# Block 0's logit sums through DRAM instead of TensorE, in a two-layer attention and GLU kernel

## The chip, the core and the metric

The kernel runs on one core of a Trainium2 chip. The metric is the device time of one execution in microseconds (us), the median of several runs. One further execution is recorded by the profiler; all traces below are of that one.

## What is computed

Two layers, with the same weights in both, on x of 2048 rows by 1024 in bfloat16. Each is an attention over a dilated window and then a gated unit:

```python
# _A_ref: H = 32 heads of Dh = 32, window W = 8, dilation 2
qkv = (x @ wqkv)                                  # split in q, k, v per head
idx = pos[:, None] - (jnp.arange(W) * 2)[None, :] # masked where idx < 0
logits = einsum("bhsd,bhswd->bhsw", q, kg) * Dh ** -0.5
o = einsum("bhsw,bhswd->bhsd", softmax(logits), vg)
return o.reshape(B, S, D) @ wo
# _B_ref: gate = x @ W_gate; up = x @ W_up
# h = (gate * (gate > 0)) * up; return h @ W_down      (F = 3584)
x = x + _A_ref(_layernorm(x)); x = x + _B_ref(_layernorm(x))     # twice
```

A logit is thus, for each row, head and one of 8 window places, a sum of 32 products q times shifted k.

## The kernel before

**Blocks.** The 2048 rows go in four blocks of 512 (b = 0 to 3, four tiles of 128 rows each). A stage of a layer is done block by block: normalize and transpose the rows (xnT, by DMA transposes on SyncE's queue, L278), project to q, k, v (`plan_proj`, L386; the projection runs weight-stationary, so its results have features on the partitions and rows along the free axis), attention on VectorE (`plan_attn`, L554), the wo product (`plan_wo`, L697) and the gated unit (`plan_gu`, L724, and `plan_down`, L765). TensorE (PE) does all large products; the attention's logits and weighted sums are done by VectorE (DVE) from copies of q, k and v that went through DRAM (q_d, k_d, v_d) and came back head-major: partition = head + 32 x tile, with the 32 features of that head and 128 rows of the tile along the free axis (qhm, khm, vhm, loaded by SyncE, L562).

**Block 0's logits of layer 0 are special** (`first_logits`, L462), since they have no time for that round trip. Its weights are read with a stride (L397), so that feature chunk c (c = 0 to 7) puts four features of each head on the partitions 4 x head to 4 x head + 3. ScalarE (ACT) copies each chunk of q and k from PSUM to q_fm and k_fm. VectorE multiplies a chunk for all 8 window places at once (`mul`, 128x4096, L496) and adds the chunks in two float32 accumulators of 128x2048, one for each half h of the window (`add`, L506). What is left is the sum over the four partitions of a head. Before the change, TensorE does it: the accumulator is split in bfloat16 terms (`split`, a cast on ScalarE, L515; `rest`, the remainder on VectorE, L528), and `red` (L537) multiplies chunk 7's product and three terms by `wide`, a 128x32 matrix of ones and zeros that GpSimd builds (L186 to L190), in 32 matmuls. ScalarE copies the sums to the logits tile L (L544). `later_hooks` sets these matmuls into block 1's projection, after the first group of ("v", 1) (L551). Then come the softmax (`soft_a`, L597, with the mask of the first rows at L601; `expo` on ScalarE, L609; `soft_b`, L611) and eight pairs of `pv_mul` and `pv_add` (L622, L631), whose outputs GpSimd (POOL) sends to o_d (L638). SyncE loads them back as oT (L646), the operand of wo.

**Order.** It is written out by a planner, not by the engines. `Plan` gives each step a planned time: TensorE's groups follow each other at 0.216 us a matmul (`on_pe`); VectorE's work is either in a chain, with a duration and a time at which it may start (`chain`), or fixed (`on_dve`), as the additions of wo's sums to x (L713) and the multiplications of the gated unit; all steps are then recorded in the order of their planned times (L119). Each engine executes its own queue strictly in that recorded order. Semaphores make what is not ready wait, and with it all that stands behind it on that engine. SyncE's queue holds weight loads, transposes and head-major loads in one line.

**Around the change.** While TensorE projects blocks 1, 2 and 3 of layer 0, VectorE does block 0's logits, softmax and weighted sums, and then block 1's logits, window place by window place (one multiply L576, three additions L586, a fold L593 and L594). `wo_hook` (L815) puts block 0's wo product into the projection of block 3, after group 2 of ("k", 0). Its eight groups of eight matmuls fill the eight PSUM buffers; VectorE adds them to x (L713), ScalarE takes sums and sums of squares of each row tile (L239, L240), VectorE and GpSimd work out mean and scale, ScalarE normalizes (L272) and SyncE transposes two row tiles at a time (L278). The result, xnT of (1, 0), is the operand of the gated unit's first group, the first work of TensorE after block 3's projection. All of block 0's gated unit needs all four row tiles of it.

**Buffers.** `ring` has five slots of 8x512 columns for weights; k's first weights fill two, the wo halves two others, and the gated unit's first gate and up weights go into slots as they come free. The pool `hm` has one buffer for each of the tags q, k and v. The tag "T" has four buffers, for xnT, for oT and for block 0's two accumulators.

Of the kernel before, what the change touches and what calls it, by code (L numbers as in the profile page):

```python
# [9 lines left out]
BF16 = mybir.dt.bfloat16  # L10
# [4 lines left out]
P = 128  # L15
D = 1024
# [107 lines left out]
def kernel(  # L124
# [42 lines left out]
    neg_half = const.tile([P, TPB], F32, name="neg_half")  # L167
    zpad = const.tile([P, KC, HALO], BF16, name="zpad")
    maskc = const.tile([32, W, HALO], F32, name="maskc")
    wide = const.tile([P, H], BF16, name="wide")  # L170
    ring = wring.tile([P, 8 * RING, SLAB], BF16, name="ring")
    q_d = [dram.tile([D, BLK], BF16, name=f"q_d{b}") for b in range(NB)]
    k_d = [dram.tile([D, ROW], BF16, name=f"k_d{b}") for b in range(NB)]
    v_d = [dram.tile([D, ROW], BF16, name=f"v_d{b}") for b in range(NB)]
    o_d = [dram.tile([TPB, H, DH, P], BF16, name=f"o_d{b}") for b in range(NB)]
    x_blk = [xpool.tile([P, TPB, D], BF16, name=f"xb{b}") if b else None for b in range(NB)]
    x_tiles = [x_blk[t // TPB][:, t % TPB, :] if t >= TPB else xpool.tile([P, D], BF16, name=f"x{t}") for t in range(NT)]
# [5 lines left out]
        nc.gpsimd.memset(neg_half[:], -0.5)  # L183

    def consts_late():
        nc.gpsimd.memset(wide[:], 1.0)  # L186
        nc.gpsimd.affine_select(out=wide[:], in_=wide[:], pattern=[[-FG, H]], compare_op=ALU.is_ge,
                                fill=0.0, base=0, channel_multiplier=1)
        nc.gpsimd.affine_select(out=wide[:], in_=wide[:], pattern=[[FG, H]], compare_op=ALU.is_ge,
                                fill=0.0, base=FG - 1, channel_multiplier=-1)  # L190
        nc.gpsimd.memset(zpad[:], 0.0)
        for t in (v_d, k_d):
            nc.gpsimd.dma_start(_dram(t[0], 0, [[ROW, P], [P * ROW, KC], [1, HALO]]), zpad[:])
        nc.gpsimd.memset(maskc[:], 0.0)
        for w in range(1, W):
            nc.gpsimd.memset(maskc[:, w, 0:DIL * w], NEG)
# [261 lines left out]

    def first_logits(st, tm):  # L462
        hold = {}
        terms = []

        def begin():
            hold["q"] = hm_pool.tile([P, KC, BLK], BF16, tag="q", name="q_fm")
            hold["k"] = hm_pool.tile([P, KC, HALO + BLK], BF16, tag="k", name="k_fm")
            nc.gpsimd.memset(hold["k"][:, :, 0:HALO], 0.0)

        def evict(nm, c, acc, t):
            def f():
                if nm == "q":
                    nc.scalar.copy(hold["q"][:, c, :], acc()[:])
                    return
                kt = hold["k"]
                nc.scalar.copy(kt[:, c, HALO:HALO + BLK], acc()[:])
                nc.gpsimd.dma_start(_dram(k_d[1], c * ROW, [[D // P * ROW, P], [1, HALO]]),
                                    kt[:, c, BLK:BLK + HALO])
            if nm == "q" and c == 0:  # L480
                plan.at(t - 1.0, begin)
            plan.at(t, f)
            if nm == "k":
                plan.chain.append((lambda: t + 0.7, 2.3, mul(c), None))
                for h in range(2 if 0 < c < KC - 1 else 0):
                    plan.chain.append((lambda: 0.0, 2.3, add(c, h), split(0, h) if c == KC - 2 else None))
                if c == KC - 1:
                    for n in range(2):
                        for h in range(2):
                            plan.chain.append((lambda n=n, h=h: tm[("split", n, h)], 2.3, rest(n, h),  # L490
                                               split(1, h) if n == 0 else (lambda now: tm.__setitem__("logits", now))))

        def mul(c):
            def f():
                pr = at_pool.tile([P, W, BLK], BF16, tag="pr", name=f"prod_{c}", bufs=2)
                nc.vector.tensor_tensor(pr[:], _ap(hold["q"], c * BLK, [[0, W], [1, BLK]]),  # L496
                                        _ap(hold["k"], c * ROW + HALO, [[-DIL, W], [1, BLK]]), op=ALU.mult)
                hold[("pr", c)] = pr
            return f

        def add(c, h):
            def f():
                if c == 1:
                    hold[("acc", h)] = tpose.tile([P, W // 2, BLK], F32, tag="T", name=f"lacc{h}")
                acc, ws = hold[("acc", h)], slice(4 * h, 4 * h + 4)
                nc.vector.tensor_tensor(acc[:], hold[("pr", 0)][:, ws] if c == 1 else acc[:], hold[("pr", c)][:, ws], op=ALU.add)  # L506
            return f

        def split(n, h):

            def f():
                if h == 0:
                    terms.append(at_pool.tile([P, W, BLK], BF16, tag="pr", name="term_0", bufs=2) if n == 0 else
                                 hm_pool.tile([P, W, BLK], BF16, tag="k", name="term_1"))
                nc.scalar.copy(terms[n][:, 4 * h:4 * h + 4], hold[("acc", h)][:])  # L515

            def after(now):
                t = max(now + 0.2, tm.get(("split", n, 0), 0.0))
                plan.at(t, f)
                tm[("split", n, h)] = t + 2.4  # L520
            return after

        def rest(n, h):
            def f():
                acc = hold[("acc", h)]
                if n == 1 and h == 0:
                    terms.append(hm_pool.tile([P, W, BLK], BF16, tag="q", name="term_2"))
                nc.vector.tensor_tensor(acc[:] if n == 0 else terms[2][:, 4 * h:4 * h + 4], acc[:],  # L528
                                        terms[n][:, 4 * h:4 * h + 4], op=ALU.subtract)
            return f  # L530

        def red():
            Ls = hold["L"] = [psum.tile([P, 4, P], F32, tag="acc", name=f"L{wh}") for wh in range(2)]
            for n, term in enumerate([hold[("pr", KC - 1)]] + terms):
                for wh in range(2):
                    for tq in range(TPB):
                        nc.tensor.matmul(Ls[wh][32 * tq:32 * tq + 32, :, :], lhsT=wide[:],  # L537
                                         rhs=term[:, 4 * wh:4 * wh + 4, tq * P:(tq + 1) * P],
                                         start=(n == 0), stop=(n == 3), skip_group_check=True, tile_position=(0, 32 * tq))

        def out():
            st["L"] = at_pool.tile([P, W, P], F32, tag="L", name="L_0_0")
            for wh in range(2):
                nc.scalar.copy(st["L"][:, 4 * wh:4 * wh + 4, :], hold["L"][wh][:])  # L544

        def step():
            e = plan.on_pe(9.5, red)
            plan.at(e + T_EV, out)
            tm["logits_in"] = e + T_EV + 1.5

        return {"evict": evict}, {("v", 1, 0): step}  # L551


    def plan_attn(L, b, ends, st, tm):  # L554
# [121 lines left out]
            plan.at(t + 0.2, expo)  # L676
            tm["exp"] = t + 2.2

        plan.chain.append(((lambda: tm["logits_in"]) if first else now, 3.0, soft_a, after_a))
        plan.chain.append((lambda: tm["exp"], 4.0, soft_b, None))  # L680

        def after_pv(t):
# [128 lines left out]
    wo_start = []  # L811
    attn = {}
    glu = {}
    later_hooks = []
    wo_hook = {("k", 0, 2): lambda: wo(0, 0)}  # L815

    def proj(L, b):
        st, tm = {}, {}
        if L == 0 and b == 0:
            hooks, later_hooks[:] = (lambda h: (h[0], [h[1]]))(first_logits(st, tm))  # L820
        else:
            hooks = later_hooks.pop() if later_hooks else wo_hook if L == 0 and b == NB - 1 else {}
        attn[(L, b)] = plan_attn(L, b, plan_proj(L, b, hooks), st, tm)

    def wo(L, b):
# [16 lines left out]
    for nm, at in (("q", -6.0), ("k", -5.5)):  # L842
        full = whole[nm].rearrange("p (c a) n -> p c (a n)", c=KC)
        hs = {"last": 0.0}
        plan.reserved.update({0: hs, 1: hs} if nm == "k" else {})
        for g in range(2):
            w0[(nm, g)] = {"t": full, "c0": g * SLAB, "all": hs, "last": 0.0}
            col0 = "qkv".index(nm) * D
            plan.at(at, lambda w=full, c=col0, a=KC // 2 * g, z=KC // 2 * (g + 1):
                    nc.sync.dma_start(w[:, a:z, :], wqkv_v[:, a:z, c:c + D]))  # L850
    w0[("v", 0)] = {"t": held[:, 2 * KC:3 * KC, :], "last": 0.0}
    for h in range(2):
        plan.at(-7.0 + 0.6 * h, lambda a=KC // 2 * h, z=KC // 2 * (h + 1):
# [2 lines left out]
    for t, at in ((1, -6.7), (2, -6.3), (3, -6.2)):  # L856
        plan.at(at, load_x(t))
    plan.at(22.0, consts_late)
    for b, n, at in ((1, 4, -5.7), (2, 4, -2.5), (3, 2, 45.0)):
        for i in range(0, TPB, n):  # L860
            plan.at(at, lambda b=b, n=n, i=i: nc.sync.dma_start(  # L861
                x_blk[b][:, i:i + n, :], _dram(x_dram, (b * BLK + i * P) * D, [[D, P], [P * D, n], [1, D]])))

    for b in range(NB):
        if b == 0:
            late_ln(0, 1, 9.0, on_vector=True)
            late_ln(0, 2, 37.0)
            late_ln(0, 3, 75.5, on_vector=True, norm_at=87.0)
        proj(0, b)
    for b in range(NB):  # L870
        if b >= 1:
# [53 lines left out]
```

## Time and profile before

| | us |
|---|---|
| median of 3 runs | 1620.91 (1620.82 to 1621.05) |
| the profiled execution, device time | 1621.7 |
| its span, first to last instruction | 1620.0 |
| TensorE (PE) busy | 1609.8 |
| VectorE (DVE) busy | 1060.6 |
| ScalarE (ACT) busy | 450.5 |
| GpSimd (POOL) busy | 111.1 |

The granted TensorE clock is 1.000 throughout. The page tells busy time over the whole span; the timelines tell, for one engine, when an instruction started, how long it took, its line and tiles, and in square brackets how long its engine stood idle before it and what ended the wait. SPq and ACTq are the queues of SyncE and ScalarE as they issue DMAs; the landing of a DMA is told by the view of a tile, as time from the issue. The chain of waits goes back from the last instruction to what released each.

### The profile page before, as it was taken

The page shows a single profiled execution, that of the slowest core. Times are in us where ns is not written, and L with a number is a line of the kernel's source. Part 1 is how long each engine was busy: PE and PEld are TensorE (multiplying, and loading weights), DVE is VectorE, ACT ScalarE, POOL GpSimd, SP SyncE. Part 2 cuts the span into 40 slices and gives each one's busy share as a digit, 9 for nine tenths or more (in the row PEclk, how much of TensorE's full clock was granted, in tenths as well). Part 3 has the DMA queues.
Part 4 walks back from the last instruction along what each step waited for, and adds up shares of the span by engine and source line. Part 5 has one row for each costly group of instructions (what it writes and reads, how often), then busy time and mean ns, then how long its engine had stood idle before and what let it go on. Part 6 is the DMA issues. An engine that isn't in the chain of part 4 may idle for free.

```text
span 1620.0 us, 19174 instructions
## 1 busy us (share of the span) xinstructions
PE 1609.8 (99%) x7609; PEld 745.5 (46%) x7658; DVE 1060.6 (65%) x1284; ACT 450.5 (28%) x707; POOL 111.1 (7%) x172
## 2 busy tenths in 40 slices
PE   8999999999999999999999999999999999999999
PEld 6444444444444444444444444444444444444444
DVE  6999989989999269960699617986989212211211
ACT  4753421304131241312413251133011311221110
POOL 3221000001010100011000110000000000000000
PEclk9999999999999999999999999999999999999999
DMA  9765878868965887668876699599846655564452
GB/s 299 162 157 136 222 197 219 189 190 216 223 181 196 231 206 206 189 204 234 198 202 195 212 240 209 159 281 225 228 155 194 184 169 163 175 186 152 156 167 68
DMA packets 443755, 314.83 MB, mean 194 GB/s; under 512 B 195568, under 2 KB 437648, under 8 KB 443664
## 3 DMA queue, kind: packets, MB, share of 16 engines
q1 hardware_dynamic: 414496, 281.39, 64.7%
q10 hardware_dynamic: 24368, 23.40, 4.4%
q0 software_dynamic: 4800, 8.80, 1.6%
q8 instruction: 60, 0.98, 0.3%
q14 instruction: 31, 0.25, 0.0%
HBM read 261.77 MB, written 36.05 MB: 184 GB/s over the span
## 4 chain that ended last, share of the span: by engine, by line
PE 98%; DMA 1%; SPq 1%; issue 0%; DVE 0%; DVEq 0%
PE acc_u L736 24%; PE acc_g L736 24%; PE dacc L782 24%; PE acc_k L401 7%; PE acc_wo L706 7%; PE acc_v L401 6%; PE acc_q L401 6%; DMA ring<-in_A_wqkv_dram 1%; SPq L850 0%; PE L L537 0%; SPq L834 0%; SPq L861 0%; DVE xb L790 0%; SPq L854 0%; SPq L838 0%
## 5 line engine op out<-in xcount | busy, mean ns | idle before, releaser
L736 PEld LDWEIGHTS <-ring 128*128 128x128 bf16 x3584 | 350.7, 98 | 422.9
L736 PE MATMUL acc_g<-xnT,ring 128*128 128x512 bf16 x1792 | 423.3, 379 | 0.0
L736 PE MATMUL acc_u<-xnT,ring 128*128 128x512 bf16 x1792 | 423.3, 379 | 0.0
L782 PE MATMUL dacc<-ring,hT 128*128 128x512 bf16 (+1 forms) x1787 | 386.4, 376 | 1.7
L751 DVE TENSOR_TENSOR hT<-acc_u,r 128x512 bf16<-128x512 f32 x224 | 154.3, 689 | 322.3 <-PE acc_u L736 316.7
L743 ACT ACTIVATE r<-acc_g 128x512 bf16<-128x512 f32 x224 | 133.6, 596 | 706.4 <-PE acc_g L736 706.4
L782 PEld LDWEIGHTS <-hT 128*128 128x128 bf16 x1820 | 178.1, 98 | 209.0
L401 PEld LDWEIGHTS <-ring 128*128 128x128 bf16 x1152 | 115.5, 100 | 134.0 <-DMA ring<-in_A_wqkv_dram 1.0
L627 DVE TENSOR_TENSOR pvt<-a,vhm 128x4096 bf16<-128x4096 bf16 x64 | 146.2, 2284 | 0.2
L586 DVE TENSOR_TENSOR l<-l,pr 128x1024 f32<-128x1024 f32 x112 | 136.8, 1221 | 2.3
L576 DVE TENSOR_TENSOR pr<-qhm,khm 128x4096 bf16<-128x4096 bf16 x56 | 127.9, 2283 | 13.1 <-DMA khm<-k_d 13.1
L401 PE MATMUL acc_k<-xnT,ring 128*128 128x512 bf16 x512 | 113.5, 379 | 0.6 <-DMA ring<-in_A_wqkv_dram 0.6
L706 PE MATMUL acc_wo<-ring,oT 128*128 128x512 bf16 x496 | 111.0, 379 | 0.8
L790 DVE TENSOR_TENSOR xb<-dacc,xb 128x512 bf16<-128x512 f32 (+1 forms) x49 | 32.6, 678 | 120.4 <-PE dacc L782 120.0
L401 PE MATMUL acc_v<-xnT,ring 128*128 128x512 bf16 x384 | 84.4, 379 | 0.0
L635 DVE TENSOR_TENSOR pvt<-pvt 128x2048 bf16<-128x2048 bf16 x64 | 78.1, 1221 | 1.3
L638 POOL DMA_DIRECT2D o_d<-ohm x64 | 35.3, 552 | 623.4 <-DVE ohm L637 612.6
L706 PEld LDWEIGHTS <-oT 128*128 128x128 bf16 x512 | 50.1, 98 | 60.4
L410 ACT CAST stage_q<-acc_q 128x512 bf16<-128x512 f32 x56 | 32.2, 583 | 148.7 <-PE acc_q L401 147.8
L586 DVE TENSOR_TENSOR l<-pr 128x1024 f32<-128x1024 bf16 x56 | 68.2, 1218 | 0.6
L593 DVE TENSOR_TENSOR l<-l 128x512 f32<-128x512 f32 x112 | 62.3, 556 | 3.0
L261 POOL TENSOR_TENSOR rstd<-vpe,neg_half 128x2 f32<-128x2 f32 x26 | 26.7, 1026 | 540.8 <-DVE vpe L260 540.6
(92 smaller groups left out, 844.9 us busy)
## 6 DMA issues: line engine op xcount, KB each, us to landing
ring<-in_B_W_gate_dram SPq DMA_DIRECT2D x56, 1024.0 KB, 7.0
ring<-in_B_W_up_dram SPq DMA_DIRECT2D x56, 1024.0 KB, 5.5
ring<-in_B_W_down_dram SPq DMA_DIRECT2D x48, 1024.0 KB, 6.1
ring<-in_A_wqkv_dram SPq DMA_DIRECT2D x27, 1024.0 KB, 5.4
ring<-in_A_wo_dram SPq DMA_DIRECT2D x16, 1024.0 KB, 7.0
vhm<-v_d SPq DMA_DIRECT2D x32, 284.0 KB, 7.0
v_d<-stage_v ACTq DMA_DIRECT2D x32, 256.0 KB, 6.0
o_d<-ohm POOLq DMA_DIRECT2D x64, 128.0 KB, 3.9
```

The costliest lines, as they stand in the source:

```text
L401: nc.tensor.matmul(acc[:, t0 * P:t1 * P], lhsT=lhsT, rhs=xnT[(L, b)][:, t0:t1, kc, :], start=(kc == 0), stop=(kc == KC - 1))
L576: nc.vector.tensor_tensor(pr[:], st["q"][:], _ap(st["k"], HALO - DIL * w, [[HALO + P, DH], [1, P]]), op=ALU.mult)
L586: nc.vector.tensor_tensor(l[:], pr[:, 0:8] if i == 0 else l[:], pr[:, 8 * i + 8:8 * i + 16], op=ALU.add)
L593: nc.vector.tensor_tensor(l[:, 0:n], l[:, 0:n], l[:, n:2 * n], op=ALU.add)
L627: nc.vector.tensor_tensor(tt[:], a_bc, v_sh, op=ALU.mult)
L635: nc.vector.tensor_tensor(tt[:, 0:4], tt[:, 0:4], tt[:, 4:8], op=ALU.add)
L638: nc.gpsimd.dma_start(_dram(o_d[b], g * DG * P, [[DH * P, P], [1, DG * P]]), o[:].rearrange("p d t -> p (d t)"))
L706: nc.tensor.matmul(acc[:], lhsT=st["oT"][:, c, t, :], rhs=ws[half]["t"][:, c, :], start=(c == 0), stop=(c == KC - 1))
L736: nc.tensor.matmul(acc[:], lhsT=w["t"][:, kc, (j % 4) * P:(j % 4 + 1) * P], rhs=xnT[(L, b)][:, :, kc, :], start=(kc == 0), stop=(kc == KC ...
L743: nc.scalar.activation(r[:], hold.pop(("g", j))[:], ACT.Relu)
L751: nc.vector.tensor_tensor(st["hT"][:, j, :], hold.pop(("u", j))[:], hold.pop(("r", j))[:], op=ALU.mult)
L782: nc.tensor.matmul(accs[(t, c0)][:], lhsT=st["hT"][:, j, t * P:(t + 1) * P], rhs=w["t"][:, jl, c0 - half * SLAB:c0 - half * SLAB + n], sta ...
```

## The change

The four additions that the matmuls with `wide` did are taken to VectorE. All eight chunks are now added in the float32 accumulators (`add` also for c = 7). SyncE stores each accumulator (1 MB) to a DRAM tile l_d and loads it back head-major in four pieces (one for each row tile: 32 partitions, four features of the head by 4 window places by 128 rows); VectorE folds the four features in two additions. `split`, `rest`, `red`, `out`, `step` and `wide` go. The loaded tiles take the buffers of the tags q and k, which the head-major q and k of block 1 use next. Besides, wo of block 0 moves from after group 2 of ("k", 0) to after group 2 of ("q", 1) in block 3's projection, k's first weights and x's last block are loaded by one DMA instead of two, and block 3's normalization is planned earlier.

```diff
-                for h in range(2 if 0 < c < KC - 1 else 0):
-                    plan.chain.append((lambda: 0.0, 2.3, add(c, h), split(0, h) if c == KC - 2 else None))
-                if c == KC - 1:
-                    for n in range(2):
-                        for h in range(2):
-                            plan.chain.append((lambda n=n, h=h: tm[("split", n, h)], 2.3, rest(n, h),
-                                               split(1, h) if n == 0 else (lambda now: tm.__setitem__("logits", now))))
+                for h in range(2 if c else 0):
+                    plan.chain.append((lambda: 0.0, 2.3, add(c, h), turn(h) if c == KC - 1 else None))
+                for h in range(2 if c == KC - 1 else 0):
+                    plan.chain.append((lambda h=h: tm[("l_in", h)], 2.0, fold(h),
+                                       (lambda now: tm.__setitem__("logits", now)) if h else None))
...
+        def turn(h):
+            def store():
+                nc.sync.dma_start(l_d[h][:], hold[("acc", h)][:])
+            def load(tq):
+                def f():
+                    if tq == 0:
+                        hold[("l", h)] = hm_pool.tile([P, FG, W // 2, P], F32, tag="qk"[h], name=f"lhm{h}")
+                    nc.sync.dma_start(hold[("l", h)][32 * tq:32 * tq + 32].rearrange("p a w t -> p (a w) t"),
+                                      _dram(l_d[h], tq * P, [[FG * W // 2 * BLK, H], [BLK, FG * W // 2], [1, P]]))
+                return f
+            def after(now):
+                plan.at(now + 0.1, store)
+                for tq in range(TPB):
+                    plan.at(now + 2.5 + 0.1 * tq, load(tq))
+                tm[("l_in", h)] = now + 11.0
+            return after
+        def fold(h):
+            def f():
+                if h == 0:
+                    st["L"] = at_pool.tile([P, W, P], F32, tag="L", name="L_0_0")
+                l = hold[("l", h)]
+                nc.vector.tensor_tensor(l[:, 0:2], l[:, 0:2], l[:, 2:4], op=ALU.add)
+                nc.vector.tensor_tensor(st["L"][:, 4 * h:4 * h + 4, :], l[:, 0], l[:, 1], op=ALU.add)
+            return f
...
-        plan.chain.append(((lambda: tm["logits_in"]) if first else now, 3.0, soft_a, after_a))
+        plan.chain.append((now, 3.0, soft_a, after_a))
...
-    wo_hook = {("k", 0, 2): lambda: wo(0, 0)}
+    wo_hook = {("q", 1, 2): lambda: wo(0, 0)}
...
+        n = KC // 2 if nm == "q" else KC
+        for a in range(0, KC, n):
+            plan.at(at, lambda w=full, c=col0, a=a, n=n:
+                    nc.sync.dma_start(w[:, a:a + n, :], wqkv_v[:, a:a + n, c:c + D]))
...
-    for b, n, at in ((1, 4, -5.7), (2, 4, -2.5), (3, 2, 45.0)):
+    for b, n, at in ((1, 4, -5.7), (2, 4, -2.5), (3, 4, 45.0)):
...
-            late_ln(0, 3, 75.5, on_vector=True, norm_at=87.0)
+            late_ln(0, 3, 70.0, on_vector=True, norm_at=78.0)
```

## The prediction

> **What bounds the kernel now.** I read the page first, then PE's waits, PE's timeline, and last the timelines of the queues that feed it. Line numbers are those of the kernel before.
>
> ```profile
> span 1620.0 us, 19174 instructions
> PE 98%; DMA 1%; SPq 1%; issue 0%; DVE 0%; DVEq 0%
> ```
>
> The chain that ended last is TensorE work for 98% of the span, so a microsecond counts only where PE issues fewer matmuls or waits. PE's waits (engine, line, releaser: total, times, longest) end early:
>
> ```profile
> PE acc_k L401 <- DMA ring<-in_A_wqkv_dram: 0.6, 1, 0.6
> ```
>
> That is the latest of five; none comes after 27 us. PE's timeline (start, length, instructions) gives the deadlines:
>
> ```profile
> 25.43 1.03 PE L401 MATMUL acc_k<-xnT,ring 128*128 128x512 bf16 x4
> 27.01 6.26 PE L401 MATMUL acc_k<-xnT,ring 128*128 128x512 bf16 x28 [0.56 <-DMA ring<-in_A_wqkv_dram]
> ...
> 150.75 13.98 PE L706 MATMUL acc_wo<-ring,oT 128*128 128x512 bf16 x62
> ...
> 193.91 1.89 PE L736 MATMUL acc_g<-xnT,ring 128*128 128x512 bf16 x8
> ```
>
> PE needs block 0's attention output oT at 150.75 and block 0's normalized, transposed rows (xnT of layer 1) at 193.91. The first oT load was issued at 141.03 and took 3.9 to land (tile view): 5.8 us to spare. The second transpose of xnT was issued at 179.14 and took 6.65: landed 185.79, 8.1 to spare. Whether the change costs time is decided at these two places. VectorE's timeline:
>
> ```profile
> 93.04 0.26 DVE L601 TENSOR_TENSOR L<-L,maskc 32x112 f32<-32x112 f32 x1
> ...
> 137.92 0.43 DVE L637 TENSOR_TENSOR ohm<-pvt 128x512 bf16<-128x512 bf16 x1
> 138.26 2.28 DVE L576 TENSOR_TENSOR pr<-qhm,khm 128x4096 bf16<-128x4096 bf16 x1
> ...
> 152.67 0.69 DVE L713 TENSOR_TENSOR x<-acc_wo,x 128x512 bf16<-128x512 f32 x1 [2.12 <-PE acc_wo L706]
> ```
>
> VectorE has no room between 93 and 138 (the windows show it busy for 42.95 of 45.30 us there), so a late start of the softmax at 93.04 arrives undiminished at 138.35. SyncE's and ScalarE's queues:
>
> ```profile
> 92.14 4.12 SPq L562 DMA_DIRECT2D qhm<-q_d  x4
> ...
> 174.40 7.52 SPq L278 DMA_TRANSPOSE xnT<-xn_all  x2
> 182.01 0.79 SPq L203 DMA_DIRECT2D ring<-in_B_W_gate_dram  x1
> 182.93 0.61 SPq L203 DMA_DIRECT2D ring<-in_B_W_up_dram  x1
> ```
>
> ```profile
> 89.18 0.37 ACTq L418 DMA_DIRECT2D v_d<-stage_v  x1
> ...
> 94.58 0.37 ACTq L418 DMA_DIRECT2D v_d<-stage_v  x1
> ...
> 177.88 1.24 ACT L272 ACTIVATE xn_all<-x,nb,rstd 128x1024 bf16<-128x1024 bf16 x1 [0.44 <-ACT stage_k L410]
> ```
>
> Two habits of these queues matter. The fourth qhm load was issued at 95.72, when the first had landed (92.14 plus 3.6): SyncE's and ScalarE's DMAs share eight completion semaphores in turn, so an issue can wait for a transfer of the other queue. And what SyncE issues lands in the order of issue.
>
> **The change, part by part.**
>
> *TensorE sums.* 32 matmuls of L537 go; the chain has them at 90.26 for 1.84 us. **-1.84**.
>
> *k in one load.* Before, half 1 let four matmuls run (25.43) ahead of half 2 (7.1 and 10.0 issue, 14.8 and 17.0 to landing: 26.97). One load of both lands no earlier than half 2, so those four run behind it: 4 x 0.216 (6.91 / 32) = **+0.86**. Bounds: 0, if the single load lands sooner by that much, to 2. PE is then 0.98 early overall.
>
> *Work that only moves.* ScalarE loses four casts of 1900 ns and two L copies, GpSimd the two selects of `wide`; VectorE loses four L528 (9.0 us) and gains two more adds of 2.25 (L506) and two folds of 1.22 + 0.69. xb3 in one load and the earlier bn_stats change order only: xb3 was there at 49.3, used at 87.2. None is worth anything by itself, since PE waited for none.
>
> *The trip through DRAM.* prod_7 ended at 78.4, now 79.2; the adds end at 81.4 and 83.7. No row shows a 1 MB store, so I bound it by 1 MB loads: 5.6 (gate at 163.03) to 7.3 (wo at 34.7), a second right behind it 2.9 to 3.9 later. Stores land about 87-89 and 90-93. Then the eight loads (256 KB of 512 B pieces; qhm has 256 B pieces, 3.6 to 4.9). By the built order the fourth load of half 0 waits for the v_d store of 89.18 (+0.86, 2.7 to landing: 92.7), and the third of half 1 for that of 94.58; the sums that delayed this store are gone, but three norms of 1.24 now stand before it in ScalarE's queue, so I leave it at 94.7. It lands 2.7 to 4.1 later, the last loads 3.6 to 4.9 after: 101.6 to 103.5. With the fold of 1.9 the softmax starts at 103.5 to 105.4 instead of 93.04: **10.5 to 12.3 late; I take 11.5.** (As planned, 11 us after the adds, it would be about 3 late; without the two waits for v_d, about 6.)
>
> *wo four groups later.* 32 matmuls move ahead of it: wo at 150.75 + 6.91 - 0.98 = 156.7. oT's first load lands at 144.9 + 11.5 = 156.4: **no wait, just**. This cover hides the late attention here, and each microsecond more is paid. khm loads, which must wait for fold 1 (its buffer), were landed at 130.5 before; VectorE wants them at 150 now.
>
> *What is late next: xnT of layer 1.* In the built order VectorE does two full rounds of block 1's logits and a multiply before the first wo add. From 138.35 + 11.5 = 149.9: two rounds of 7.49 (138.26 to 145.75) and 2.28 make 167.1; PE had the sum at 158.4. Eight adds at 0.61, three l at 1.2, a fold 1.4, small operations 0.65: the last add ends at 177.8 (165.5 before). ScalarE behind it, in its order: statistics 2.4, five casts at 0.57, three DMA issues at 0.5, four norms at 1.2: row pair 1 normalized at 185.3, pair 2 at 189.4. SyncE's order is now transpose 1, gate, up, transpose 2 (before: both transposes first). Gate is issued at 187.6; the pair gate/up took 182.01 to 194.05 before, so up lands at about 199.6. Transpose 2 waits besides for ScalarE's k_d store, issued at about 188, which with weights in flight takes 4.7 to 7.6 (rows at 180.9, 184.4), so it is issued at 193 to 195.6, and lands 2.3 (35.4 to 37.7 for the first pair) to 3.9 (181.9 to 185.8) behind up: 202 to 203.5. I take 203. PE wants it at 192.9: **+10.1**.
>
> Sum: 1621.7 - 1.84 + 0.86 + 10.1 = 1630.8 for the profiled execution; that lies 0.8 over the median shown (1620.91), so **1630.0**. Nothing behind gives it back or adds: PE has no idle time to take it from, and the next deadline (oT of block 1, last load landed 291.9, its row tile wanted 10.4 after 291.0) has 9.5 to spare, while PE is late too.
>
> **A rule against this.** The Trainium skill ("DMA: Bandwidth & Descriptors", Queues, rings and completion order) says that completion is not FIFO per issuing engine. Here the trace disagrees so far: all SyncE landings up to 260 us are in the order of issue. If the rule held for transpose 2, the fourth rival below would be the result.
>
> **Rivals.**
> - *Longer trip.* 512 B pieces are slow, the logits come 6 us later still. For: 256 KB loads took up to 9.5 under traffic. Then oT comes 5.7 after PE wants it, and the xnT wait stays about 10: 1636. ScalarE, whose exponential waits for VectorE in its queue, would then also hold evictions.
> - *Not slower: the trip is short.* If the logits arrive by 94.7, the plan's time, the softmax is only 3 late, the first add at 158.6 meets PE's 158.4, and transpose 2 waits only for gate and up, issued at 179: landing near 193. Time 1621.7 - 0.98 = 1620.7, so 1620 in the median. It decides at about 3 us of lateness. Against it: the two waits for v_d stores, which both queues' order fixes. The Trainium skill ("DMA: Bandwidth & Descriptors", Anatomy of one DMA, a fit for GpSimd's path) gives 2.0 us plus bytes over 436 GB/s: by that estimate a store takes 4.4 and the trip would come nearer to this rival. Rows of 5.6 to 7.3 here are longer.
> - *k load.* If it lands 2 us later than its second half did, 2 more: 1632.
> - *Transpose 2 passes the weights.* It lands 3.9 after its issue of 193 to 195.6 plus 2.8: about 199, a wait of 6: 1626.
> - *No effect of the form claimed* (the sums stay) is excluded by the built order.
>
> **How the numbers follow.** Forecast (1627 to 1633.5): 0.60, the k load's case within it. Transpose 2 earlier (1624 to 1627): 0.10. Longer trip (1633.5 to 1640): 0.16. Short trip (1619.5 to 1623): 0.12. Faster, if the single k load also lands early: 0.02; the most that can go is 1.84 + 0.56 = 2.4, under 0.2% (3.2 us, about what a measurement tells from no change). Range 1623.5 to 1637: leaves out the short trip and a quarter of the longer. Slower 0.86, same 0.12, faster 0.02.
>
> **What would show it.** PE's waits: one of about 10 us for xnT before the first acc_g, near 203, none or under 1 before acc_wo. VectorE's timeline: softmax at 103.5 to 105, two waits for lhm before it, first wo add near 167 with no wait for PE. ScalarE: about 9 us before the exponential. SyncE: gate and up between the transposes. I am wrong if the softmax starts before 97, or if transpose 2 lands by 193.

## The result, and the profile after

The changed kernel takes 1640.3 us in the median (1638.12 to 1640.47, 4 runs), against 1620.98 for the kernel before beside it (1620.82 to 1622.01): a ratio of 1.0115, with a 95% interval of 1.0097 to 1.0132. It is 19.3 us slower. The forecast was 1630.0, range 1623.5 to 1637.0: the sign was right, about half of the loss was foreseen, and the result lies 3.3 above the range. Line numbers from here on are those of the kernel after. Two lines of its page, the span and the chain by engine:

```profile
span 1638.8 us, 19168 instructions
PE 93%; DMA 3%; DVE 3%; issue 0%; SPq 0%; ACT 0%; DVEq 0%; ACTq 0%
```

The chain has left TensorE for 7% of the span; before it was 2%. PE's waits (engine, line, releaser: total, times, longest) say where:

```profile
PE acc_g L714 <- issue: 8.6, 1, 8.6
PE acc_wo L684 <- DMA oT<-o_d: 2.9, 1, 2.9
PE acc_k L396 <- DMA ring<-in_A_wqkv_dram: 2.4, 1, 2.4
PE acc_q L396 <- ACT stage_q L405: 1.6, 1, 1.6
```

Four waits, 15.5 us, where the kernel before had one of 0.56 after the start. "issue" at the first acc_g means that the view names no releaser; a transfer does it, as the landings below show. The wait for stage_q is ScalarE's doing: it copies PE's results out of the PSUM buffers, and it stood still ahead of the exponential, which stands before those copies in its queue and waits for VectorE's late softmax:

```profile
113.90 1.06 ACT L587 ACTIVATE L<-L 128x1024 f32<-128x1024 f32 x1 [13.14 <-DVE L L584]
```

PE's timeline (start, length, instructions, and the idle time ahead) holds a second price:

```profile
27.35 8.81 PE L396 MATMUL acc_k<-xnT,ring 128*128 128x512 bf16 x32 [2.35 <-DMA ring<-in_A_wqkv_dram]
115.48 5.34 PE L396 MATMUL acc_q<-xnT,wqv 128*128 128x512 bf16 x24 [1.61 <-ACT stage_q L405]
163.42 15.68 PE L684 MATMUL acc_wo<-ring,oT 128*128 128x512 bf16 x64 [2.89 <-DMA oT<-o_d]
210.18 3.57 PE L714 MATMUL acc_g<-xnT,ring 128*128 128x512 bf16 x8 [8.63 <-issue]
```

Groups of 32 take 7.07 elsewhere and groups of 8 take 1.89. Behind three of the four waits they take longer: 1.74 at 27.35, 1.70 at 163.42 (against 13.98 before), and 1.68 plus 0.86 in the two groups from 210.18; none behind the wait of 1.61. The windows (stretch: length, busy times and instructions of PE, PEld, DVE, ACT and POOL, then granted clock, DMA share, GB/s) name the reason, a granted clock of 0.50, low already while PE still waits and back at 1.00 some microseconds later:

```profile
206.00:210.00 4.00, 0.00 (x0) 0.00 (x0) 2.83 (x3) 0.00 (x0) 0.00 (x0) 0.50 1.14 273
210.00:212.00 2.00, 1.82 (x5) 0.72 (x6) 0.00 (x0) 0.00 (x0) 0.00 (x0) 0.50 0.79 274
216.00:218.00 2.00, 2.00 (x11) 0.89 (x10) 1.60 (x2) 0.00 (x0) 0.00 (x0) 1.00 0.00 0
```

The chain that ended last, in the stretch of the change (start, length, what):

```profile
97.05 3.27 DMA v_d<-stage_v
100.33 0.54 SPq L509
100.92 7.61 DMA lhm<-l_d
108.84 1.24 DVE lhm L525
...
159.19 4.18 DMA oT<-o_d
163.42 15.68 PE acc_wo L684 x64
...
194.16 11.70 DMA ring<-in_B_W_up_dram
210.18 3.57 PE acc_g L714 x8
```

Read from the top: a store of block 1's v holds the issue of the third load of half 1 until 100.32, the last load lands at 108.53, the fold and the softmax follow, oT comes 2.89 after PE wanted it. Lower down stands the up slab: it lands at 205.85, and the second transpose behind it. SyncE's timeline shows these four in their order:

```profile
191.04 1.98 SPq L273 DMA_TRANSPOSE xnT<-xn_all  x1
193.11 0.94 SPq L198 DMA_DIRECT2D ring<-in_B_W_gate_dram  x1
194.16 1.04 SPq L198 DMA_DIRECT2D ring<-in_B_W_up_dram  x1
198.45 7.14 SPq L273 DMA_TRANSPOSE xnT<-xn_all  x1
```

By the landings, that transpose arrived at 210.09, where PE was free at 201.55. And VectorE, at the two places by which the prediction wanted to be judged:

```profile
110.83 0.27 DVE L579 TENSOR_TENSOR L<-L,maskc 32x112 f32<-32x112 f32 x1
...
173.12 1.28 DVE L691 TENSOR_TENSOR x<-acc_wo,x 128x512 bf16<-128x512 f32 x2
```

The softmax begins at 110.83 (93.04 before, 103.5 to 105.4 forecast), and the first wo add at 173.12 (167.1 forecast), without waiting for PE. The waits, the half clock and the matmuls removed account for the span: 2.89 lost around k (PE's next group starts at 36.00 instead of 33.11), -1.84, 1.61, 2.89 + 1.70, 8.63 + 2.54 make 18.4 of the 18.8 by which it grew.

### The profile page after: what moved, and what is told of

It is laid out like the page before. It is cut to its first block, busy times and chain, and to the rows that moved or that the text cites. A ratio compares the mean times of both kernels' runs of the same rounds, so it can differ in the third digit from the quotient of the medians.

```text
span 1638.8 us, 19168 instructions
## 1 busy us (share of the span) xinstructions
PE 1617.9 (99%) x7626; PEld 746.9 (46%) x7626; DVE 1059.2 (65%) x1286; ACT 440.5 (27%) x701; POOL 104.2 (6%) x169
## 4 chain that ended last, share of the span: by engine, by line
PE 93%; DMA 3%; DVE 3%; issue 0%; SPq 0%; ACT 0%; DVEq 0%; ACTq 0%
PE acc_g L714 24%; PE acc_u L714 24%; PE dacc L760 24%; PE acc_wo L684 7%; PE acc_k L396 6%; PE acc_q L396 5%; PE acc_v L396 5%; DMA ring<-in_A_wqkv_dram 1%; DVE pvt L605 1%; DMA ring<-in_B_W_up_dram 1%; DVE pvt L613 1%; DMA lhm<-l_d 0%; DVE pvt L614 0%; DMA oT<-o_d 0%; DVE ohm L615 0%
## 5 line engine op out<-in xcount | busy, mean ns | idle before, releaser
L396 PEld LDWEIGHTS <-wqv 128*128 128x128 bf16 x480 | 44.8, 104 | 41.6 <-issue 2.6
```

The lines of the kernel that those rows point to most:

```text
L396: nc.tensor.matmul(acc[:, t0 * P:t1 * P], lhsT=lhsT, rhs=xnT[(L, b)][:, t0:t1, kc, :], start=(kc == 0), stop=(kc == KC - 1))
```

## The experiments

**Theory:** three things make the loss. The logits' trip is longer than forecast, because SyncE's issues wait for ScalarE's stores; the order that comes with wo's new place puts gate and up ahead of the second transpose; and a PE wait of more than about 2 us is paid again in half clock. **Rivals:** bandwidth, not waiting, makes the trip long; the trip alone is guilty and the order harmless; one of the terms hides the other. Differences between runs are of their medians; taken against the kernel before that ran beside each, those from the changed kernel shift by up to 0.4.

**k in two loads**, as before:

```diff
-        n = KC // 2 if nm == "q" else KC
+        n = KC // 2
```

> The changed kernel with k's first weights in two loads again. Theory (the trip's length and the waits it makes, and every longer PE wait paid a second time by a slow clock): the wait of 2.35 us at 27.35 and the 1.74 us that its first 32 matmuls took longer shrink to the 0.56 of before, and VectorE's logit rounds start as much earlier, so everything behind moves with it: 1640.3 - 2.9 = 1637.4. Rival (only the late xnT of layer 1 counts, and what the k load costs is hidden behind it): 1640.3.

Measured: 1637.6, ratio 1.0104 (1.0089 to 1.0119): 2.7 less than the changed kernel, though the runs of the two overlap (1636.74 to 1639.93). The profile has the four matmuls ahead of the second half again, and a wait of 1.65 without a slow group behind it.

**The trip left out**: store and loads go, and fold reads the accumulators.

```diff
-                plan.at(now + 0.1, store)
-                for tq in range(TPB):
-                    plan.at(now + 2.5 + 0.1 * tq, load(tq))
...
-                l = hold[("l", h)]
+                l = hold[("acc", h)][:].rearrange("p w (a t) -> p a w t", a=FG)
```

> The changed kernel without the ten DMAs of the trip: fold reads the accumulators where they lie, so the logits are not turned to head-major rows (that part of the computation is left out). The order of all else is that of the changed kernel. Theory (the trip makes the loss): softmax near 90 instead of 110.8, no wait for acc_q, oT or xnT: 1640.3 - 1.6 - 2.9 - 1.7 - 8.6 - 2.5 = 1623.0. Rival (the new order of work, gate and up between the transposes and wo later, costs by itself): 1627 or more, with a wait before the first acc_g.

Measured: 1628.42, ratio 1.0051 (1.0034 to 1.0068). My 1623 missed; the rival's figure came. The trip costs 11.9, and 7.8 of loss stay although the softmax begins at 94.51. One of PE's timeline lines shows what stays:

```profile
197.60 3.57 PE L711 MATMUL acc_g<-xnT,ring 128*128 128x512 bf16 x8 [4.63 <-DMA xnT<-xn_all]
```

**wo back at its old place**, the rest as in the changed kernel:

```diff
-    wo_hook = {("q", 1, 2): lambda: wo(0, 0)}
+    wo_hook = {("k", 0, 2): lambda: wo(0, 0)}
...
-            t = max(t + 5.0, st["wo_at"] - 30.0)
+            t = max(t + (3.0 if first else 5.0), st["wo_at"] - 30.0)
```

> The changed kernel with wo(0,0) back at group (k,0,2) (the oT loads of block 0 are planned 2 us earlier so that they stand ahead of it); with it both transposes stand ahead of the second gate and up again. Theory (the oT time and the place of the transposes set the end, wo's place only says where PE waits): oT lands at about 163.4 as in the changed kernel, PE waits about 10 there, the wait at the first acc_g is under 2: 1636 to 1639. Rival (the four groups hide what the prediction said they hide, each microsecond of wo earlier is paid): 1640.3 + 6.9 = 1647.

Measured: 1633.84, ratio 1.0080 (1.0065 to 1.0095), 6.5 better than with wo later and more than I expected. PE waits 9.2 for oT, about as computed, but not at all at the first acc_g. The place that was to hide late attention made it dearer.

**k in one load, alone**, in the kernel before:

```diff
-            plan.at(at, lambda w=full, c=col0, a=KC // 2 * g, z=KC // 2 * (g + 1):
-                    nc.sync.dma_start(w[:, a:z, :], wqkv_v[:, a:z, c:c + D]))
+        n = KC // 2 if nm == "q" else KC
+        for a in range(0, KC, n):
+            plan.at(at, lambda w=full, c=col0, a=a, n=n:
+                    nc.sync.dma_start(w[:, a:a + n, :], wqkv_v[:, a:a + n, c:c + D]))
```

> The kernel before with one edit: k's first weights in one 2 MB load. Theory (wait plus slow clock): the load lands near 27.3, a wait of about 2 before the first acc_k and about 1.7 of slow clock behind it, nothing of it given back: 1621.0 + 2.9 = 1623.9. Rival (the prediction's step: four matmuls run later, no more): 1621.9.

Measured: 1621.65 (1620.99 to 1625.03, 10 runs), ratio 1.0006 (0.9997 to 1.0016). That is 1.0 more, and the interval leaves anything from no cost to 2.6: the rival's 0.86 fits, the theory's 2.9 does not. In the profiled execution the load landed at 25.34 and PE waited 0.40. Over the profiles with one load it landed between 25.34 and 27.91, the second of two between 25.77 and 27.42: no later on the whole. What one load costs is the four matmuls that could run ahead, and a wait long enough, now and then, to meet the half clock: of the ten executions the one of 1625.03 alone has a mean granted clock of 0.999, the others 1.000. Of the seven profiles with one load, the changed kernel's alone has half clock there, and PE's next group starts latest in it (36.00; 32.35 to 34.92 in the others).

**wo later, alone**, in the kernel before:

```diff
-    wo_hook = {("k", 0, 2): lambda: wo(0, 0)}
+    wo_hook = {("q", 1, 2): lambda: wo(0, 0)}
```

> The kernel before with one edit: wo(0,0) four groups later, at (q,1,2). By the planned order this also puts the second gate and up between the two transposes of xnT and two rounds of block 1's logits ahead of the first wo add. Theory (that order costs by itself): first add near 160, the second transpose waits behind gate and up and lands 4 to 6 us after PE wants it at 193.9, and the clock is slow behind that wait: 1621 + 5 to 8.5 = 1626 to 1629.5. Rival (wo later is free where oT is early): 1621.

Measured: 1628.21, ratio 1.0043 (1.0028 to 1.0058): 6.8 lost, with the softmax where it always was. SyncE's timeline:

```profile
180.85 1.92 SPq L278 DMA_TRANSPOSE xnT<-xn_all  x1
182.86 1.42 SPq L203 DMA_DIRECT2D ring<-in_B_W_gate_dram  x1
184.38 0.64 SPq L203 DMA_DIRECT2D ring<-in_B_W_up_dram  x1
185.15 9.13 SPq L278 DMA_TRANSPOSE xnT<-xn_all  x1
```

The issue of the second transpose alone takes 9.13 here, and it lands at 198.52, behind up at 194.58; PE waits 4.24 and loses another 1.7 at half clock. The rival "wo later is free" falls.

**The weights behind the transposes**, the rest as in the changed kernel:

```diff
+                start = plan.pe - 24.0 if (L, b, j) == (1, 0, 4) else -10.0
-                sl = {"g": slab(wg_v[:, :, c0:c0 + SLAB], f"wg_{L}_{b}_{j // 4}"),
-                      "u": slab(wu_v[:, :, c0:c0 + SLAB], f"wu_{L}_{b}_{j // 4}")}
+                sl = {"g": slab(wg_v[:, :, c0:c0 + SLAB], f"wg_{L}_{b}_{j // 4}", start),
+                      "u": slab(wu_v[:, :, c0:c0 + SLAB], f"wu_{L}_{b}_{j // 4}", start)}
```

> The changed kernel with the second gate and up of block 0 given a start time, so that SyncE issues both transposes of xnT first; VectorE's order is unchanged. Theory (the weights in front of the second transpose make the wait of 8.6 us and the 2.5 us of slow clock): the transpose lands at 200 to 202 instead of 210.1, the wait is under 1: 1629 to 1630.5. Rival (the transpose is late because the wo adds and norms are late): it lands at 206 or later, and the time stays at 1636 or more.

Measured: 1629.43, ratio 1.0055 (1.0040 to 1.0070): 10.9 less than the changed kernel, nearly all by the order of four DMA issues. (By the profiles, 9.7 of it is at the first acc_g; 1.9 come from a shorter wait for k's weights, which no edit made, and wo loses 1.3 more to its wait and the half clock behind it.) The wo adds are nearly as late (170.97 to 181.36, against 173.12 to 183.51), yet the second transpose lands at 202.04. PE's timeline:

```profile
202.18 1.89 PE L714 MATMUL acc_g<-xnT,ring 128*128 128x512 bf16 x8 [1.43 <-DMA xnT<-xn_all]
```

The wait fell from 8.63 to 1.43, and the group behind it runs at full clock. The order of the issues, not the late norms, made that wait. The edit also freed the transpose of the k_d store, which held it until 198.38 in the changed kernel, 3.5 after its rows were normalized (194.87), so this run doesn't tell the two apart; in the run before, no store held the transpose, and the weights alone made a wait of 4.24.

**One load of 1 MB for each half**, instead of four:

```diff
-                    nc.sync.dma_start(hold[("l", h)][32 * tq:32 * tq + 32].rearrange("p a w t -> p (a w) t"),
-                                      _dram(l_d[h], tq * P, [[FG * W // 2 * BLK, H], [BLK, FG * W // 2], [1, P]]))
+                    nc.sync.dma_start(hold[("l", h)][:].rearrange("p a w t -> p (a w) t"),
+                                      _dram(l_d[h], 0, [[P, TPB], [FG * W // 2 * BLK, H], [BLK, FG * W // 2], [1, P]]))
```

> The changed kernel with each half's logits fetched by one load of 1 MB instead of four of 256 KB: the same 512 B pieces, but two issues on SyncE instead of eight, so none has to wait for ScalarE's v_d stores. Theory (those waits, 8.1 us together, make half of the trip's length): softmax at 103 to 106 instead of 110.8, everything behind as much earlier: 1633.5 to 1636. Rival (the pieces themselves are slow and the queue is full): softmax at 110 or later, 1640.

Measured: 1656.96, ratio 1.0222 (1.0207 to 1.0237). Both expectations missed. The softmax begins at 126.38; half 0, issued at 85.83, is there only at 108.85, when the fold starts. The windows (columns as above) show a mostly idle transfer system meanwhile:

```profile
104.00:108.00 4.00, 4.00 (x20) 1.83 (x19) 0.00 (x0) 0.00 (x0) 0.00 (x0) 1.00 0.30 68
```

A share of 0.30 is about 5 of 16 DMA engines. The trace bears out that few carry such a load: its completion semaphore is stepped four times as the first one lands (107.22 to 108.83), that of each 256 KB load in the trace after 16 times. That the outer dimension of 4 sets this is my reading; no run varied it alone. The run tells nothing on the waits.

**The loads on GpSimd**, still four to a half:

```diff
-                    nc.sync.dma_start(hold[("l", h)][32 * tq:32 * tq + 32].rearrange("p a w t -> p (a w) t"),
+                    nc.gpsimd.dma_start(hold[("l", h)][32 * tq:32 * tq + 32].rearrange("p a w t -> p (a w) t"),
```

> The changed kernel with the eight logit loads issued by GpSimd instead of SyncE, so they share no completion semaphore with ScalarE's stores; GpSimd's halo stores and the rstd of block 3 now stand behind loads that wait for the store of the accumulators. Theory (shared semaphores make the trip long): softmax at 103 to 106: 1633.5 to 1636. Rival (bandwidth, or GpSimd's queue held up instead): softmax at 110 or later, 1640 or more.

Measured: 1634.17, ratio 1.0083 (1.0066 to 1.0100), 6.1 less. From VectorE's timeline, the two folds:

```profile
95.92 1.23 DVE L525 TENSOR_TENSOR lhm<-lhm 128x1024 f32<-128x1024 f32 x1 [0.31 <-DMA lhm<-l_d]
102.04 1.22 DVE L525 TENSOR_TENSOR lhm<-lhm 128x1024 f32<-128x1024 f32 x1 [4.17 <-DMA lhm<-l_d]
```

All eight are issued by 91.76 (101.66 on SyncE), the last lands at 101.96 instead of 108.53, and the softmax begins at 104.02. Single transfers are not quicker (median 8.1 from issue to landing, 5.5 on SyncE); they are no longer held back. Not all of the 6.8 by which the softmax came earlier is due to that: 2.9 are there at the accumulators already, complete at 82.78 instead of 85.71, as k's weights landed earlier in this execution (26.07 instead of 27.31) and no half clock followed. From the last add to the softmax, the four profiles with the loads on SyncE took 24.9 to 25.3, the four with the loads on GpSimd (this one and three below) 19.6 to 21.2. So the waits cost 4 to 5 of the trip's 25; the rest is there without them, and for that the rival of slow transfers stands. oT comes in time for wo; the wait at acc_g grows to 11.8, because the order is still the bad one and PE is early.

**The mends together**: the three diffs of k in two loads, the loads on GpSimd, and the weights behind.

> Three mends of the changed kernel together: k's first weights in two loads, the logit loads on GpSimd, the second gate and up behind both transposes. Theory (lateness of the logits from shared semaphores, plus weights in front of the second transpose): wo at 156 without a wait, first add near 166, second transpose landed at 194 to 196, where PE wants xnT at 192: a wait of 2 to 4 with up to 3 of slow clock: 1621 to 1626. Rival (the two terms overlap, one hides the other): 1629, as with the weights behind alone.

Measured: 1623.93 (1620.39 to 1625.70, 11 runs), ratio 1.0017 (1.0008 to 1.0026). Apart, the three gained 2.7, 6.1 and 10.9, which makes 19.7; together they gain 16.4. Most of it adds, and the rival's 1629 falls. In the profiled execution (1621.72) the wait for xnT is 1.62, with full clock behind it. The longer executions have no profile, but the mean granted clock of each is on record: 1.000 in the four up to 1623.47, 0.999 in the seven from 1623.50 on. One stretch of 3.41 us at 0.50 makes that difference; that it lies behind this wait is an inference.

**And the wo adds one round of logits earlier** on VectorE:

```diff
+            held = 8.0 if (L, b) == (0, 1) else 0.0
...
-            return tm["qk_in"]
+            return tm["qk_in"] if not held else max(tm["qk_in"], prev[-1]["pv"] + held)
...
-            t = max(t + 5.0, st["wo_at"] - 30.0)
-            step = 1.2 if first else PIECE
+            second = (L, b) == (0, 1)
+            t = max(t + (2.0 if second else 5.0), st["wo_at"] - 30.0)
+            step = 1.2 if first or second else PIECE
```

> As the kernel with the three mends, and VectorE does one round of block 1's logits ahead of the first wo add instead of two and a multiply (the planner holds block 1's rounds back by 8 us, and its oT loads are planned closer together). Theory: first add near 158.5, second transpose landed by 190, no wait for xnT: 1618.5 to 1620.5, which is the gain of the matmuls removed and nothing else. Rivals: the wait stays as without this edit (the norms, not the adds, are late): 1621 to 1626; block 1's attention, 5 us later, makes a wait at wo(0,1) near 291: over 1624.

Measured: 1619.46 (1618.86 to 1620.49, 11 runs), ratio 0.9991 (0.9982 to 1.0000). This version is 1.35 below the kernel before, under 0.1%, and the interval just reaches no difference. VectorE's and PE's timelines:

```profile
157.71 0.68 DVE L693 TENSOR_TENSOR x<-acc_wo,x 128x512 bf16<-128x512 f32 x1
```

```profile
155.54 13.98 PE L686 MATMUL acc_wo<-ring,oT 128*128 128x512 bf16 x62
191.80 1.89 PE L716 MATMUL acc_g<-xnT,ring 128*128 128x512 bf16 x8
```

No wait at wo, none at acc_g, although the softmax still begins 9.9 later than before the change (102.91).

**No trip, wo at its old place, k in two loads**: what the change could bring at most (the edits of three experiments above together).

> The changed kernel without the ten DMAs of the trip (fold reads the accumulators where they lie: the turn to head-major rows is left out), with wo(0,0) back at (k,0,2) and k's weights in two loads: what is left is the kernel before without its 32 matmuls of sums. Theory (all of the loss is trip and order): no wait of PE after 30 us, 1621.0 - 1.84 = 1619.2. Rival (something else that the change moved costs too): over 1621.

Measured: 1619.33, ratio 0.9990 (0.9981 to 0.9999), against 1619.2 expected. Nothing else that was moved costs; the matmuls are worth 1.5.

**GpSimd loads with wo at its old place**, to price wo's place once the transposes stand first (again the edits of three experiments above):

> The changed kernel with k's weights in two loads, the logit loads on GpSimd, and wo(0,0) back at (k,0,2), which also puts both transposes ahead of the second gate and up. Theory (wo later does hide late attention, once the transposes stand first): oT lands at 155 to 157 where PE wants it at 149: a wait of 6 to 8 and up to 3 of slow clock, none at the first acc_g: 1625 to 1630, 4 or more above the kernel with wo at (q,1,2) and the weights behind. Rival (wo's place is worth nothing, xnT sets the end either way): the two are equal within 2.

Measured: 1627.32, ratio 1.0039 (1.0026 to 1.0051), with one wait:

```profile
PE acc_wo L684 <- DMA oT<-o_d: 5.0, 1, 5.0
```

and 2.7 lost to the half clock behind it. With wo later and the weights behind it was 1623.93. So wo's later place hides 3.4 of late attention, if the transposes don't pay for it; I had expected 4 or more, and a wait of 6 to 8.

## Why the prediction fell short

| term | forecast | in the profile after | what the runs say |
|---|---|---|---|
| TensorE sums gone | -1.84 | -1.84 | -1.5 with the trip left out, -1.35 with all else mended |
| k in one load | +0.86 | +1.15, +1.74 half clock | 1.0 alone, 2.7 within the change |
| held evictions (acc_q) | 0 | +1.61 | 1.4 to 1.8 with a softmax at 108.5 to 110.8, none at 104.0 or earlier |
| wo waits for oT | 0 | +2.89, +1.70 half clock | none with the loads on GpSimd and wo later |
| first acc_g waits for xnT | +10.1 | +8.63, +2.54 half clock | 1.43 at full clock when the weights went behind |

**The step that failed is the trip through DRAM**: "10.5 to 12.3 late; I take 11.5" was 17.8. Three parts were short. The accumulators were complete at 85.7 and not at 83.7. I had let VectorE's chain of products move 0.8 with the k load (79.2 instead of 78.4), but its first product waits for the first acc_k, which the wait for the load and the half clock behind it made late, and came 2.8 later. Before and after:

```profile
28.75 2.29 DVE L496 TENSOR_TENSOR prod<-q_fm,k_fm 128x4096 bf16<-128x4096 bf16 x1 [2.76 <-ACT k_fm L477]
```

```profile
31.56 2.29 DVE L487 TENSOR_TENSOR prod<-q_fm,k_fm 128x4096 bf16<-128x4096 bf16 x1 [5.71 <-ACT k_fm L470]
```

The stores landed within the stretches estimated (87.51 and 92.43) although they began 2 later; they took 4.0 and 6.7. Of the loads, I let the fourth of half 0 wait for one v_d store; the third waited for that one (issued 88.62, landed 93.98), and the fourth for the next, until 97.28. And the store that holds the third of half 1, left at 94.7, was issued at 97.05, behind the three norms that I had set against the sums removed. SyncE's waits have the three together:

```profile
SPq L509 <- DMA v_d<-stage_v: 8.1, 3, 4.4
```

And a load in that crowd took 3.8 to 7.6, not 3.6 to 4.9. From the last add to the softmax I had 20.8 and it took 25.1. With the 2.0 of the accumulators, that is the 6.3 by which 11.5 fell short. On GpSimd's queue, where no store of ScalarE's holds an issue, this way took 19.6 to 21.2; my aside that without the two waits the softmax would be about 6 late allowed it 15.3, so the transfers were priced too low as well. (The terms given make 101.0 to 103.7 for the last loads, not 101.6 to 103.5; that changes nothing.)

**The xnT step was right in mechanism**: gate and up between the transposes, the second transpose held by a k_d store (landed 198.38), landing behind the weights. That its size came near is in part luck: the transpose landed 7.1 later than the 203 written, as the softmax was 6 later, and PE was 8.7 later too, so that the wait was 8.6 and not 10.1. The second step that failed is what this wait was put down to. I made it hang on the late softmax and treated wo four groups later as a cover; alone, with the softmax on time, wo's move loses 6.8.

**Half clock was in no term.** It made 5.98 of the 18.8 in the profiled execution. Without it the forecast's own rival, a longer trip with the logits 6 later (1636), would have been the result to within 2 us, if with other shares (it had 5.7 for the wait for oT, which was 2.9); it named the late oT and ScalarE's held evictions (the copies out of PSUM), and had 0.16.

**The rivals.** The short trip fell with the waits for v_d, as argued. But its time was wrong too: it had 1620 for a softmax about 3 late, and the two runs with wo at its new place and the softmax 0.3 and 1.5 late (93.34, wo alone; 94.51, no trip) took 1628.2 and 1628.4. It had gate issued at 179 and transpose 2 landed near 193; gate was issued at 182.86 and 180.53, up landed at 194.58 and 193.03, and the transpose about 4 behind it. That transpose 2 passes the weights fell (its terms also make 199.7 to 202.3, not 199): in the trace after and in those of all experiments, no transfer whose landing the trace has landed before one that the same queue issued ahead of it (420 of SyncE's in the trace after). The Trainium skill ("DMA: Bandwidth & Descriptors", Queues, rings and completion order) says that completion is not FIFO per issuing engine; in these traces it was.

## What to carry to other kernels

Moving a consumer later to cover a late producer also moves everything that is planned from it: look at which transfers the new order puts in front of its results, because the order of four DMA issues cost more here (about 10) than the microseconds that the move hid (3.4). When a transfer is added, follow the completion semaphores of each of its issues to the queues that share them, and charge the stores of the other engine with the work that stands before them. Charge a wait of TensorE of more than about 2 us with a second sum for the clock (1.5 to 3.0 here), and add up what the change can gain at most before its costs: here 1.8 us against a trip of some 25, from the last add (85.7) to the softmax (110.83).

## What the hardware showed beyond expectation

The clock: over all traces, 14 waits of 0.9 to 2.1 us (from 25 us on) cost nothing behind them; waits of 2.35, 2.59, 2.89 and 2.96 cost 1.7, 1.5, 1.7 and 3.0 in matmuls of 0.43 instead of 0.216, one of 2.65 nothing; nine of 4.2 to 19.3 cost 1.5 to 2.8, with no relation to their length. After a wait of 4.24 the first four matmuls ran at full rate and the slow ones came behind them. The traces' record of the granted clock accounts for this. Its low stretches last 3.41 us or a whole number of times that, and in one trace they begin on one grid of 3.41 (in the trace after at 27.53, 164.06 and 205.02, which are 40 and 12 steps apart). From full clock, a step at half followed every step in which PE stood idle for 2.13 us or more, and none in which it did for 1.79 or less; the wait of 2.65 lies across two steps, with 1.74 and 0.91. The cost is half of what is left of the low stretch when PE works again: behind the wait of 8.63 the last 5.08 of 10.24, so 2.54. The Trainium skill ("TensorE: Matmul & The Clock Gate", Part 1) tells of a gate that halves the clock and looks at windows of about 3.4 us that run free of the program, which fits the rates and the grid; that a gap must exceed 3.4 us to count, as its section on oscillation has it, the wait of 2.35 contradicts.

Transposes by DMA: while weights were in flight, the issue of the second one took 6.7 to 9.1 us on SyncE in five traces; the first, ahead of those weights, 1.9 to 2.2 in the same traces. And one transfer of 1 MB in 512 B pieces took 23 us at a DMA share of 0.30, where four of 256 KB kept the share near 1.
